# Attention with a block mask, then a gMLP: q and k transposed by TensorE into tiles whose mask rows stay, with earlier loads

## The chip, the core and the metric

The kernel runs on one core of a Trainium2 chip. The metric is the device time of one execution in microseconds, as the median of several executions. The core has five engines that run their own instruction streams in program order and meet through semaphores: TensorE (PE for its matmuls, PEld for its weight loads), VectorE (DVE), ScalarE (ACT), GpSimd (POOL) and SyncE (SP), which computes nothing here and issues most of the DMAs. Matmul results land in PSUM; the other tiles lie in SBUF. DMAs are issued from the queues of SP, ACT and POOL.

## The reference, cut to what matters

```python
# q, k, v: (4, 8, 768, 64) float32; sampled_blocks: (24, 3) integers
def _attn_ref(q, k, v, sampled_blocks):
    scores = scale * np.matmul(q, k.transpose(0, 1, 3, 2))     # scale = 1/8
    mask = np.abs(blk_i - blk_j) <= 1                          # blocks of 32 positions
    mask = mask | (blk_i == 0) | (blk_j == 0) | (blk_i == 23) | (blk_j == 23)
    for qb in range(24):
        for kb in sampled_blocks[qb]:
            mask[qb*32:(qb+1)*32, kb*32:(kb+1)*32] = True
    scores = np.where(mask, scores, -1e9)
    attn = softmax(scores)
    return np.matmul(attn, v)

def _moe_ref(x, w_in, w_spatial, b_spatial, w_out):            # x: (4, 768, 512), heads side by side
    h = np.maximum(x @ w_in, 0.0)                              # w_in: (512, 1024)
    u, v = h[..., :512], h[..., 512:]
    v_n = (v - mean(v)) / np.sqrt(var(v) + 1e-06)
    v_s = w_spatial @ v_n + b_spatial[None, :, None]           # w_spatial: (768, 768)
    return (u * v_s) @ w_out                                   # w_out: (512, 512)
```

The output is float32 of shape (4, 768, 512).

## The kernel before

Batches and heads are worked through in 16 pairs of heads (`NP`), four pairs a batch. A head has 768 positions, in 6 chunks (`NCH`) of 128. The main loop runs over pairs `p` and 12 steps `s`, six a head. A step emits `qk_exp`: two matmuls of 384 columns for the scores of one chunk of keys against all queries (L235), and one exponential by ScalarE out of PSUM (L239). Seven steps later (`LAG`) comes `av` for the same place: six matmuls of 65 columns (L251), the 65th column giving the sum of the exponentials. At a head's last chunk `norm` divides (VectorE, L264 and L265). Scores have two PSUM buffers (tag `sc`), so TensorE can be one step ahead of ScalarE.

The mask is made by the matmul itself. A contraction row is 88 long (`KR`): 64 of the head and 24, one a block of keys. On the k side, these 24 are 1 in the key's own block; on the q side they are 0 where the query's block may see the key's block and -300 where not. Before the change, they stand as columns behind the 64 of `nat_k` and `nat_q`, two tiles of each of [position, head, chunk, 128 columns], filled once: `key_blocks` (L169, L171) on POOL, `query_blocks` (L202) on VectorE.

For each pair, at step 0 of the pair before it, the loop emits: the loads of the pair after (`load`, L96; SP's queue, float32 staging tiles `st_q`, `st_k`, `st_v` with two buffers each), the casts to bfloat16 on POOL (`cast_qk`, L104, and `cast_v`, L113), and for k and for q one DMA transpose on SP's queue (`tr_dma`, L118), which turns the whole of `nat` into `t_k` or `t_q` with the contraction on the partitions. Pair 0 alone is transposed on TensorE (`tr_first`, L207 to L212). All three weights are loaded on POOL's queue at pair 0's step 0 (L430, L432, L434).

After step 8 of the next pair, `xtr` transposes a pair's normalized output to `xt`: by a DMA transpose on SP (L278), for the last pair of a batch on TensorE with a copy by VectorE (L274, L276). Then the batch's gMLP is queued as 24 units (`moe_units`), spread over the next 48 steps by a budget: six `v_unit` (L323; VectorE evicts at L329 and takes statistics at L332 and L333), six `u_unit` (L346), six `s_unit` (L368; a DMA transpose of `gn` to `gt` on SP behind each) and six `o_unit` (L386), whose results go to `osb`, four buffers, copied by ScalarE (L391) or VectorE (L393) in turn, and from there to the output by a DMA on SP (L394). Units use PSUM tag `moe`, two buffers, as do the transposes on TensorE. For the last batch the units run one after the other behind the loop. In pairs 2 and 3, six `wspt_unit` transpose the spatial weights (L287).

What sets the order is the program's own: each engine's queue has its instructions in the order in which the loop emits them, and an instruction that waits holds all that is behind it on its queue, DMAs on SP too.

Of the kernel before, what the change touches and what calls it, by code (L numbers as in the profile page):

```python
# [12 lines left out]
I32 = mybir.dt.int32  # L13
# [13 lines left out]
def kernel(  # L27
# [49 lines left out]

    nat = {nm: [const.tile([128, 2, NCH, 128], BF16, name=f"nat_{nm}{i}") for i in range(2)]
           for nm in "qk"}
# [12 lines left out]
    def load(p, names="qkv"):  # L92
        b, g = divmod(p, NG)
        for nm, src in (("q", q), ("k", k), ("v", v)):
            if nm in names:
                nc.sync.dma_start(out=st_tile(p, nm), in_=dram(src, b, 2 * g, 2))  # L96

    def cast_qk(p, nm, h, eng):
        src = st[nm, p][:, h].rearrange("p (c d) -> p c d", d=D)
        dst = nat[nm][p % 2][:, h, :, 0:D]  # L100
        if eng is nc.scalar:
            nc.scalar.activation(out=dst, in_=src, func=AF.Copy)
        else:
            eng.tensor_copy(out=dst, in_=src)  # L104
# [12 lines left out]
    def tr_dma(p, nm):  # L117
        nc.sync.dma_start_transpose(  # L118
            out=t_tile(p, nm).rearrange("x h (c n) -> x (h c) n", c=NCH),
            in_=nat[nm][p % 2].rearrange("p h c x -> p (h c x)"))  # L120
# [8 lines left out]
    load(0, "v")  # L129
    load(1)  # L130
    nc.sync.dma_start(out=b_col, in_=moe_b_spatial.rearrange("(p c) -> p c", c=NCH))

    nc.vector.memset(warm, 0.0)
# [32 lines left out]
    def key_blocks(i):  # L166
        x = nat["k"][i][:, :, :, D:KR]
        pat = [[0, 2], [1, NCH], [-BLK, NB]]
        nc.gpsimd.affine_select(out=x, in_=x, compare_op=ALU.is_ge, fill=0.0, base=0,  # L169
                                pattern=pat, channel_multiplier=NCH)  # L170
        nc.gpsimd.affine_select(out=x, in_=x, compare_op=ALU.is_ge, fill=0.0,  # L171
                                base=BLK - 1, pattern=[[0, 2], [-1, NCH], [BLK, NB]],
                                channel_multiplier=-NCH)

    key_blocks(0)
# [16 lines left out]
    cast_qk(0, "q", 0, nc.vector)  # L192
    cast_qk(0, "k", 0, nc.scalar)

    mq = psum.tile([128, 512], FP32, tag="av", bufs=2, name="mq")
    mq = mq[:, 0:NCH * NB].rearrange("p (c b) -> p c b", b=NB)
    for c in range(NCH):
        nc.tensor.matmul(out=mq[:, c, :], lhsT=ind[:, c * 128:(c + 1) * 128], rhs=bm,
                         start=True, stop=True)

    def query_blocks(i, h):
        nc.vector.tensor_copy(out=nat["q"][i][:, h, :, D:KR], in_=mq)  # L202

    def tr_first(h, nm, copy):
        ps = psum.tile([128, S], BF16, tag="moe", bufs=2)
        for c in range(NCH):
            nc.tensor.transpose(out=ps[:, c * 128:(c + 1) * 128], in_=nat[nm][0][:, h, c, :],  # L207
                                identity=ident)
        copy(qkt[nm, 0][0:KR, h, :], ps[0:KR, :])
# [20 lines left out]
    def qk_exp(j, ci):  # L230
# [3 lines left out]
        for hf in range(2):  # L234
            nc.tensor.matmul(out=ps[:, hf * 512:hf * 512 + HALF],  # L235
                             lhsT=qkt["k", j // 2][0:KR, j % 2, ci * 128:(ci + 1) * 128],
                             rhs=qkt["q", j // 2][0:KR, j % 2, hf * HALF:(hf + 1) * HALF],
                             start=True, stop=True)
# [65 lines left out]
    def moe_units(b):  # L304
# [75 lines left out]
        for tcc in range(NCH):  # L380
            def o_unit(tcc=tcc):
# [7 lines left out]
                osb = work.tile([128, DM], FP32, tag="osb", bufs=4)  # L389
# [15 lines left out]
    for p in range(NP + 1):  # L405
        for s in range(12):
# [6 lines left out]
            if p == 0 and s == 1:  # L413
                tr_first(1, "k", dve_copy)
                tr_first(1, "q", dve_copy)
            if s == 0 and p < NP:
                if p == 0:
                    cast_v(0)
                if p + 2 < NP:
                    load(p + 2)  # L420
                if p + 1 < NP:
                    if p == 0:
                        key_blocks(1)
                    for nm in "kq":
                        for h in range(2):
                            cast_qk(p + 1, nm, h, nc.gpsimd)
# [62 lines left out]
```

## Time and profile before

| what | us |
|---|---|
| median of 3 runs (265.31 to 266.99) | 265.33 |
| the profiled execution | 264.3 |
| its span, first to last instruction | 262.6 |
| PE busy | 221.6 |
| ACT busy | 171.6 |
| PEld busy | 131.1 |
| DVE busy | 103.8 |
| POOL busy | 57.3 |

A profile is of one execution. An engine's busy time says nothing of what it waits for: for this, the profile has a list of waits (who waited for whom), a timeline, and the chain of work that ended last. In rows of the timeline the numbers are the start and the length in us; then come the engine, the line, the operation, the output and inputs by the program's names, the shapes and how many were merged; in square brackets stands how long the engine was idle before, and what ended this. "SPq" is SP's queue of DMA issues, and its length that of issuing, not of moving the data.

### The profile page before, as it was taken

Reading aid. Unit: us, or ns where it says so; the run is one execution under the profiler, and the core shown is the slowest. Engines: PE = TensorE matmul, PEld = TensorE weight load, DVE = VectorE, ACT = ScalarE, POOL = GpSimd, SP = SyncE. Lnnn points to the kernel's source line nnn. Section 1 sums busy time; section 2 is a strip of 40 time slices with the busy share of each in tenths; the row PEclk is TensorE's granted clock in tenths of the full one; section 3 lists DMA queues with packets and bytes.
Section 4 is the critical chain, followed back from the end, with each engine's and each line's share of the span. In section 5 each row is a group of like instructions: output and inputs, shape, how many; then the busy total and the mean of one; then the engine's idle time right before and its main releaser. Section 6 shows DMA issues by size and latency. Waiting matters only on the chain.

```text
span 262.6 us, 5197 instructions
## 1 busy us (share of the span) xinstructions
PE 221.6 (84%) x2090; PEld 131.1 (50%) x2090; DVE 103.8 (40%) x228; ACT 171.6 (65%) x244; POOL 57.3 (22%) x116
## 2 busy tenths in 40 slices
PE   5880049999899999996699999993999999989994
PEld 1540026667656655563365655561455655544451
DVE  7500011323289324321487233330496233349442
ACT  3590029999977986786178976783279967526441
POOL 5761004304403520404015302104015000003000
PEclk9776557999999999999599999998599999999998
DMA  6499999999990957979972939789954332740006
GB/s 200 160 272 165 191 262 158 265 241 196 276 284 13 244 108 195 199 178 218 335 180 40 272 73 263 120 218 260 307 108 79 73 72 40 116 184 15 0 5 235
DMA packets 84379, 44.77 MB, mean 170 GB/s; under 512 B 67844, under 2 KB 80644, under 8 KB 84228
## 3 DMA queue, kind: packets, MB, share of 16 engines
q1 hardware_dynamic: 82832, 41.30, 66.4%
q0 software_dynamic: 1200, 2.75, 6.0%
q10 hardware_dynamic: 324, 0.39, 0.5%
q8 instruction: 16, 0.26, 0.4%
q14 instruction: 7, 0.06, 0.1%
HBM read 24.38 MB, written 6.29 MB: 117 GB/s over the span
## 4 chain that ended last, share of the span: by engine, by line
PE 62%; DMA 16%; ACT 8%; SPq 7%; POOL 2%; issue 2%; DVE 1%; POOLq 0%; DVEq 0%; ACTq 0%
PE ps L235 18%; PE ps_av L251 9%; PE ps_moe L368 9%; ACT a_all L239 8%; PE ps_moe L323 7%; DMA t_q<-nat_q 6%; PE ps_moe L346 6%; SPq L118 5%; DMA st_k<-in_k_dram 5%; PE ps_moe L386 3%; DMA out_dram<-osb 3%; DMA st_v<-in_v_dram 2%; PE ps_t L368 2%; PE ps_t L386 1%; PE ps_t L346 1%
## 5 line engine op out<-in xcount | busy, mean ns | idle before, releaser
L239 ACT ACTIVATE a_all<-ps 128x768 bf16<-128x768 f32 x192 | 144.5, 810 | 64.3 <-PE ps L235 63.8
L235 PE MATMUL ps<-t_q,t_k 88*128 88x384 bf16 x384 | 99.1, 342 | 23.6 <-DMA t_q<-nat_q 17.6
L251 PEld LDWEIGHTS <-a_all 128*128 128x128 bf16 x1152 | 64.2, 101 | 35.7 <-issue 5.3
L251 PE MATMUL ps_av<-vv,a_all 128*128 128x65 bf16 x1152 | 70.0, 197 | 0.0
L235 PEld LDWEIGHTS <-t_k 88*128 88x128 bf16 x384 | 29.4, 101 | 29.5 <-issue 26.3
L104 POOL CAST nat_k<-st_k 128x384 bf16<-128x384 f32 x30 | 14.5, 512 | 86.5 <-DMA st_k<-in_k_dram 64.9
L264 DVE RECIPROCAL rc<-ps_av 128x6 f32<-128x6 f32 x32 | 6.0, 186 | 63.2 <-PE ps_av L251 63.2
L323 PE MATMUL ps_moe<-w_in_t,xt 128*128 128x512 bf16 x72 | 21.1, 420 | 10.1 <-DVE osb L393 10.1
L371 DVE SCALAR_TENSOR_TENSOR gn<-ps_moe,b_col,un 128x512 bf16<-128x512 f32 x18 | 13.5, 750 | 32.7 <-PE ps_moe L368 32.7
L368 PE MATMUL ps_moe<-vn,w_spt 128*128 128x512 bf16 x108 | 26.3, 378 | 0.0
L368 PEld LDWEIGHTS <-w_spt 128*128 128x128 bf16 x144 | 13.8, 97 | 14.3
L323 PEld LDWEIGHTS <-xt 128*128 128x128 bf16 x96 | 9.9, 103 | 21.5 <-issue 13.2
L336 POOL TENSOR_SCALAR std<-mv 128x3 f32<-128x3 f32 x8 | 1.9, 242 | 83.5 <-DVE mv L333 72.1
L346 PE MATMUL ps_moe<-w_in_t,xt 128*128 128x512 bf16 x72 | 18.5, 378 | 0.0
L386 PE MATMUL ps_moe<-w_out_t,gt 128*128 128x512 bf16 x72 | 18.5, 378 | 0.0
L265 DVE TENSOR_TENSOR xn<-ps_av,rc 128x384 bf16<-128x384 f32 x32 | 17.8, 557 | 1.1
L332 DVE BATCH_NORM_STATS2 stats<-vsb 128x6 f32<-128x512 bf16 x24 | 16.7, 694 | 1.4 <-ACT vsb L327 0.8
L113 POOL CAST vv<-st_v 128x768 bf16<-128x768 f32 x16 | 13.5, 842 | 13.1 <-DMA st_v<-in_v_dram 8.3
L393 DVE COPY osb<-ps_moe 128x512 f32<-128x512 f32 x9 | 6.2, 691 | 25.4 <-PE ps_moe L386 13.3
L329 DVE TENSOR_SCALAR vsb<-ps_moe 128x512 bf16<-128x512 f32 x18 | 12.3, 684 | 7.9 <-PE ps_moe L323 7.9
L104 POOL CAST nat_q<-st_q 128x384 bf16<-128x384 f32 x30 | 14.4, 507 | 0.0
L346 PEld LDWEIGHTS <-xt 128*128 128x128 bf16 x96 | 9.3, 97 | 9.5
(80 smaller groups left out, 139.5 us busy)
## 6 DMA issues: line engine op xcount, KB each, us to landing
st_v<-in_v_dram SPq DMA_DIRECT2D x16, 384.0 KB, 5.1
out_dram<-osb SPq DMA_DIRECT2D x24, 256.0 KB, 2.1
st_q<-in_q_dram SPq DMA_DIRECT2D x15, 384.0 KB, 3.6
st_k<-in_k_dram SPq DMA_DIRECT2D x15, 384.0 KB, 4.3
ws_nat<-in_moe_w_spatial_dram POOLq DMA_DIRECT2D x1, 1152.0 KB, 12.5
w_in_t<-in_moe_w_in_dram POOLq DMA_DIRECT2D x1, 1024.0 KB, 17.5
w_out_t<-in_moe_w_out_dram POOLq DMA_DIRECT2D x1, 512.0 KB, 20.1
st_k<-in_k_dram ACTq DMA_DIRECT2D x2, 192.0 KB, 4.8
```

The source lines that it names most:

```text
L104: eng.tensor_copy(out=dst, in_=src)
L113: nc.gpsimd.tensor_copy(out=vv[p % 3][:, :, :, 0:D], in_=st.pop(("v", p)).rearrange("p h (c d) -> p h c d", d=D))
L235: nc.tensor.matmul(out=ps[:, hf * 512:hf * 512 + HALF], lhsT=qkt["k", j // 2][0:KR, j % 2, ci * 128:(ci + 1) * 128], rhs=qkt["q", j // 2][ ...
L239: nc.scalar.activation(out=a_ref[j][:, ci, :].rearrange("p (b c) -> p b c", b=2), in_=ps.rearrange("p (b c) -> p b c", b=2)[:, :, 0:HALF], ...
L251: nc.tensor.matmul(out=av_ref[j][:, qc, :], lhsT=a_ref[j][:, ci, qc * 128:(qc + 1) * 128], rhs=vv[p % 3][:, h, ci, :], start=(ci == 0), st ...
L265: nc.vector.tensor_tensor(out=xn_ref[p][:, :, h, :], in0=ps[:, :, 0:D], in1=rc.to_broadcast([128, NCH, D]), op=ALU.mult)
L323: nc.tensor.matmul(out=ps, lhsT=xt(g)[:, tcc * 128:(tcc + 1) * 128], rhs=w_in_t[:, g, DH:DFF], start=(g == 0), stop=(g == NDM - 1))
L332: nc.vector.bn_stats(out=stats, in_=vsb[:, tcc, :])
L346: nc.tensor.matmul(out=ps, lhsT=xt(g)[:, tcc * 128:(tcc + 1) * 128], rhs=w_in_t[:, g, 0:DH], start=(g == 0), stop=(g == NDM - 1))
L368: nc.tensor.matmul(out=ps, lhsT=w_spt[:, sc, tcc * 128:(tcc + 1) * 128], rhs=vn[:, sc, :], start=(sc == 0), stop=(sc == NCH - 1))
L371: nc.vector.scalar_tensor_tensor(out=gn[:, tcc, :], in0=ps, scalar=b_col[:, tcc:tcc + 1], in1=un[:, tcc, :], op0=ALU.add, op1=ALU.mult)
L386: nc.tensor.matmul(out=ps, lhsT=gt[:, tcc, dhc, :], rhs=w_out_t[:, dhc, :], start=(dhc == 0), stop=(dhc == NDH - 1))
```

## The change

- q and k of pairs 1 to 15 are transposed by TensorE. `tr_pair` does it for one pair and one of k and q: six transposes of [128 positions, two heads of 64], one a chunk, into one PSUM tile of tag `moe`, and two copies by VectorE of 64 partitions x 768, one a head. They are emitted at steps 5 (k) and 9 (q) of the pair before.
- `qt` and `kt` are four standing tiles each of 88 partitions, used in turn by head. Their last 24 partitions hold the mask and are written once: `kt`'s are the block indicators `ind`, `qt`'s are computed by two matmuls of 384 columns and copied by ScalarE; six copies by VectorE (`second_head`) bring both to the other three tiles. `nat` shrinks to the 64 columns of two heads side by side and loses its mask columns, their memsets, `key_blocks` and `query_blocks`.
- One cast on POOL takes both heads of q or k (`prepare`, with `cast_v`). It is emitted two pairs ahead at step 7, and the loads on SP three pairs ahead at step 7.
- The weights are issued on POOL at three places of the loop: `ws_nat` in pair 0 behind the casts of pair 1, `w_in_t` behind those of pair 2, `w_out_t` behind those of pair 3.
- `osb` has six buffers instead of four, `xt` eight instead of ten. The sampled blocks are loaded ahead of k of pair 0. One unit that is left at the loop's end runs ahead of the last `xtr`, not behind it.

```diff
-    nat = {nm: [const.tile([128, 2, NCH, 128], BF16, name=f"nat_{nm}{i}") for i in range(2)]
-           for nm in "qk"}
+    qt = [const.tile([KR, S], BF16, name=f"qt{s}") for s in range(4)]
+    kt = [const.tile([KR, S], BF16, name=f"kt{s}") for s in range(4)]
...
-    def load(p, names="qkv"):
+    def load(p, names="qkv", eng=nc.sync):
...
+                eng.dma_start(out=st_tile(p, nm), in_=dram(src, b, 2 * g, 2))
+
+    nat = {}
+
+    def nat_tile(p, nm):
+        nat[nm, p] = work.tile([128, NCH, 2, D], BF16, tag=f"nat_{nm}", bufs=2,
+                               name=f"nat_{nm}")
+
+    def cast_qk(p, nm, hs, eng):
+        src = st[nm, p][:, hs].rearrange("p h (c d) -> p h c d", d=D)
+        dst = nat[nm, p].rearrange("p c h d -> p h c d")[:, hs]
...
-    qkt = {}
-
-    def t_tile(p, nm):
-        qkt[nm, p] = work.tile([128, 2, S], BF16, tag=f"t_{nm}", bufs=3, name=f"t_{nm}")
-        return qkt[nm, p]
...
-    def tr_dma(p, nm):
-        nc.sync.dma_start_transpose(
-            out=t_tile(p, nm).rearrange("x h (c n) -> x (h c) n", c=NCH),
-            in_=nat[nm][p % 2].rearrange("p h c x -> p (h c x)"))
+    def prepare(p):
+        for nm in "kq":
+            nat_tile(p, nm)
+            cast_qk(p, nm, slice(0, 2), nc.gpsimd)
+        cast_v(p)
...
+    nc.scalar.dma_start(out=samp_i, in_=_listify(sampled_blocks).bitcast(I32))
     nc.scalar.dma_start(out=stk[:, 0:1], in_=dram(k, 0, 0, 1))
-    nc.scalar.dma_start(out=samp_i, in_=_listify(sampled_blocks).bitcast(I32))
...
-    for i in range(2):
-        nc.vector.memset(nat["k"][i][:, :, :, D:KR], 1.0)
-        for nm in "kq":
-            nc.vector.memset(nat[nm][i][:, :, :, KR:128], 0.0)
-        if i == 0:
-            nc.scalar.activation(out=tiny, in_=tiny, func=AF.Exp)
...
-    def key_blocks(i):
-        x = nat["k"][i][:, :, :, D:KR]
-        pat = [[0, 2], [1, NCH], [-BLK, NB]]
...
-    key_blocks(0)
...
+    nat_tile(0, "q"), nat_tile(0, "k")
+    cast_qk(0, "q", slice(0, 1), nc.vector)
+    cast_qk(0, "k", slice(0, 1), nc.scalar)
+    nc.vector.tensor_copy(out=kt[0][D:KR, :], in_=ind)
+
+    mq = psum.tile([128, 1024], FP32, tag="sc", bufs=2, name="mq")
+    for hf in range(2):
+        nc.tensor.matmul(out=mq[0:NB, hf * 512:hf * 512 + HALF], lhsT=bm,
+                         rhs=ind[:, hf * HALF:(hf + 1) * HALF], start=True, stop=True)
+    nc.scalar.activation(out=qt[0][D:KR, :].rearrange("p (b c) -> p b c", b=2),
+                         in_=mq[0:NB].rearrange("p (b c) -> p b c", b=2)[:, :, 0:HALF],
+                         func=AF.Copy)
...
+    def tr_head(h, nm, copy):
...
+            nc.tensor.transpose(out=ps[0:D, c * 128:(c + 1) * 128], in_=nat[nm, 0][:, c, h],
                                 identity=ident)
-        copy(qkt[nm, 0][0:KR, h, :], ps[0:KR, :])
-
-    def dve_copy(o, i):
-        nc.vector.tensor_copy(out=o, in_=i)
-
-    def act_copy(o, i):
-        nc.scalar.activation(out=o, in_=i, func=AF.Copy)
-
-    t_tile(0, "q"), t_tile(0, "k")
-    query_blocks(0, 0)
-    tr_first(0, "k", act_copy)
-    tr_first(0, "q", dve_copy)
-    cast_qk(0, "k", 1, nc.vector)
-    cast_qk(0, "q", 1, nc.vector)
-    query_blocks(0, 1)
-    query_blocks(1, 0)
-    query_blocks(1, 1)
+        copy((qt if nm == "q" else kt)[h][0:D, :], ps[0:D, :])
+
+    def tr_pair(p, nm):
+        src = nat.pop((nm, p))
+        ps = psum.tile([128, S], BF16, tag="moe", bufs=2)
+        for c in range(NCH):
+            nc.tensor.transpose(out=ps[:, c * 128:(c + 1) * 128],
+                                in_=src[:, c].rearrange("p h d -> p (h d)"), identity=ident)
+        for h in range(2):
+            nc.vector.tensor_copy(out=(qt if nm == "q" else kt)[(2 * p + h) % 4][0:D, :],
+                                  in_=ps[h * D:(h + 1) * D, :])
+
+    tr_head(0, "q", dve_copy)
+    tr_head(0, "k", dve_copy)
+
+    def second_head():
+        cast_qk(0, "k", slice(1, 2), nc.vector)
+        cast_qk(0, "q", slice(1, 2), nc.vector)
+        for sl in range(1, 4):
+            nc.vector.tensor_copy(out=kt[sl][D:KR, :], in_=kt[0][D:KR, :])
+            nc.vector.tensor_copy(out=qt[sl][D:KR, :], in_=qt[0][D:KR, :])
...
-                             lhsT=qkt["k", j // 2][0:KR, j % 2, ci * 128:(ci + 1) * 128],
-                             rhs=qkt["q", j // 2][0:KR, j % 2, hf * HALF:(hf + 1) * HALF],
+                             lhsT=kt[j % 4][:, ci * 128:(ci + 1) * 128],
+                             rhs=qt[j % 4][:, hf * HALF:(hf + 1) * HALF],
...
-        xt_ref[p] = work.tile([128, S], BF16, tag="xt", bufs=10, name="xt")
+        xt_ref[p] = work.tile([128, S], BF16, tag="xt", bufs=8, name="xt")
...
-                osb = work.tile([128, DM], FP32, tag="osb", bufs=4)
+                osb = work.tile([128, DM], FP32, tag="osb", bufs=6)
...
-            if p == 0 and s == 1:
-                tr_first(1, "k", dve_copy)
-                tr_first(1, "q", dve_copy)
-            if s == 0 and p < NP:
+            if p == 0 and s == 0:
+                second_head()
+            if p == 0 and s == 2:
+                tr_head(1, "k", dve_copy)
+                tr_head(1, "q", dve_copy)
+            if p + 1 < NP and s in (5, 9):
+                tr_pair(p + 1, "kq"[s // 8])
+            if p == 0 and s == 0:
+                cast_v(0)
+                prepare(1)
+                load(2)
+                nc.gpsimd.dma_start(out=ws_nat,
+                                    in_=moe_w_spatial.rearrange("(p c) s -> p c s", c=NCH))
+            if s == 7 and p + 2 < NP:
+                if p + 3 < NP:
+                    load(p + 3)
+                prepare(p + 2)
                 if p == 0:
-                    cast_v(0)
-                if p + 2 < NP:
-                    load(p + 2)
-                if p + 1 < NP:
-                    if p == 0:
-                        key_blocks(1)
-                    for nm in "kq":
-                        for h in range(2):
-                            cast_qk(p + 1, nm, h, nc.gpsimd)
-                        tr_dma(p + 1, nm)
-                    cast_v(p + 1)
-                if p == 0:
-                    nc.gpsimd.dma_start(out=ws_nat,
-                                        in_=moe_w_spatial.rearrange("(p c) s -> p c s", c=NCH))
                     nc.gpsimd.dma_start(out=w_in_t,
                                         in_=moe_w_in.rearrange("(g p) f -> p g f", p=128))
+                if p == 1:
                     nc.gpsimd.dma_start(out=w_out_t,
...
+    if moe_q:
+        moe_q.popleft()[1]()
     xtr(NP - 1)
     moe_q.extend(moe_units(B - 1))
```

Three places show how the instructions move. The first is SP's queue at the start, behind the loads of pairs 0 and 1 (the numbers are the tiles' own). Before:

```order
L96 DMA st_q_201<-in_q_dram 128x2x384
L96 DMA st_k_203<-in_k_dram 128x2x384
L96 DMA st_v_205<-in_v_dram 128x2x384
L118 DMA_TRANSPOSE t_k_211<-nat_k1_77 128x12x128
L118 DMA_TRANSPOSE t_q_215<-nat_q1_75 128x12x128
L96 DMA st_q_318<-in_q_dram 128x2x384
```

After the change, on the same queue and at the same place:

```order
L95 DMA st_q_202<-in_q_dram 128x2x384
L95 DMA st_k_204<-in_k_dram 128x2x384
L95 DMA st_v_206<-in_v_dram 128x2x384
L95 DMA st_q_263<-in_q_dram 128x2x384
L95 DMA st_k_265<-in_k_dram 128x2x384
L95 DMA st_v_267<-in_v_dram 128x2x384
```

The loads of pair 3 now follow those of pair 2 directly, without a transpose between them.

The second is SP's queue in pair 8, where the first batch's outputs stand. Before:

```order
L394 DMA out_0_dram<-osb_1565 128x512
L96 DMA st_q_1579<-in_q_dram 128x2x384
L96 DMA st_k_1581<-in_k_dram 128x2x384
L96 DMA st_v_1583<-in_v_dram 128x2x384
L118 DMA_TRANSPOSE t_k_1587<-nat_k1_77 128x12x128
L118 DMA_TRANSPOSE t_q_1591<-nat_q1_75 128x12x128
L394 DMA out_0_dram<-osb_1599 128x512
```

After the change, on the same queue in the same pair:

```order
L371 DMA_TRANSPOSE gt_1000<-gn_999 128x4x128
L390 DMA out_0_dram<-osb_1682 128x512
L390 DMA out_0_dram<-osb_1701 128x512
L390 DMA out_0_dram<-osb_1734 128x512
L390 DMA out_0_dram<-osb_1762 128x512
L390 DMA out_0_dram<-osb_1800 128x512
L95 DMA st_q_1816<-in_q_dram 128x2x384
```

Five outputs now follow one another, and the pair's loads come behind the fifth instead of the first.

The third is VectorE's queue in pair 4, from the last `xt` copy of the first batch to its first v_unit. Before:

```order
L264 RECIPROCAL rc<-ps_av 128x6
L265 TENSOR_TENSOR xn<-ps_av,rc 128x6x64
L276 COPY xt<-ps 128x768
L329 TENSOR_SCALAR vsb<-ps_moe 128x512
L332 BN_STATS stats<-vsb 128x6
```

After the change, on the same queue:

```order
L260 RECIPROCAL rc<-ps_av 128x6
L261 TENSOR_TENSOR xn<-ps_av,rc 128x6x64
L272 COPY xt<-ps 128x768
L210 COPY qt_76<-ps 64x768
L210 COPY qt_77<-ps 64x768
L325 TENSOR_SCALAR vsb<-ps_moe 128x512
```

Two copies of q of pair 5 now stand between the `xt` copy and the first v_unit's eviction.

More of the change, by code (lines that the diff above doesn't have):

```diff
@@ L128 @@
         nc.sync.dma_start(out=stq[:, h:h + 1], in_=dram(q, 0, h, 1))
-    load(0, "v")
-    load(1)
+    load(0, "v", nc.sync)
+    load(1, "qkv", nc.sync)
     nc.sync.dma_start(out=b_col, in_=moe_b_spatial.rearrange("(p c) -> p c", c=NCH))
-    nc.vector.memset(warm, 0.0)
     ind_nat = const.tile([NB, S], BF16)
@@ L140 @@
     nc.vector.memset(tiny, 0.0)
[L141 to L146 removed]
+    nc.vector.memset(warm, 0.0)
+    nc.scalar.activation(out=tiny, in_=tiny, func=AF.Exp)
     wps = psum.tile([128, 512], FP32, tag="moe", bufs=2)
@@ L191 @@
     nc.vector.tensor_copy(out=ind, in_=ind_nat.rearrange("b (p c) -> b c p", c=NCH))
[L192 to L208, printed above, removed]
-        copy(qkt[nm, 0][0:KR, h, :], ps[0:KR, :])
+    nat_tile(0, "q"), nat_tile(0, "k")
[9 more added lines that the diff above has]
+                         func=AF.Copy)
     def dve_copy(o, i):
```

12 lines of the change are left out of this document (3 added, 9 removed).

## The prediction

> **What bounds the kernel now.** I read the list of waits first, then the busy time by stage, then the timeline at the three places that these two point to. The list of waits (waiting line, releaser: total us, times, longest):
>
> ```profile
> PE ps L235 <- DMA t_q<-nat_q: 17.6, 2, 17.5
> DVE osb L393 <- DMA out_dram<-osb: 12.1, 2, 6.2
> PE ps_moe L323 <- DVE osb L393: 10.1, 2, 5.2
> ```
>
> TensorE stands still once for 17.5 us until a transposed q has landed, and twice for about 5 us behind a VectorE copy that waits for an output transfer. The stages (columns: stretch, its length, busy us and instructions of PE, PEld, DVE, ACT, POOL, granted TensorE clock, DMA share, GB/s), cut where a pair's first exponential starts:
>
> ```profile
> 18.89:37.37 18.48, 1.00 (x12) 0.57 (x9) 0.00 (x0) 0.81 (x2) 0.83 (x1) 0.58 1.14 191
> 37.37:65.73 28.36, 26.93 (x333) 19.03 (x331) 7.99 (x19) 26.66 (x37) 8.07 (x15) 0.91 1.08 224
> 65.73:112.95 47.22, 45.77 (x473) 27.86 (x472) 21.85 (x47) 38.94 (x55) 12.97 (x24) 1.00 0.78 186
> 112.95:132.55 19.60, 14.70 (x137) 8.52 (x135) 6.03 (x12) 10.09 (x15) 2.63 (x5) 0.83 1.00 256
> 132.55:169.98 37.43, 36.69 (x369) 21.88 (x366) 17.86 (x39) 30.14 (x43) 10.25 (x19) 1.00 0.70 156
> 169.98:190.22 20.24, 15.05 (x137) 8.54 (x136) 6.03 (x12) 10.09 (x15) 2.64 (x5) 0.83 0.99 254
> 190.22:227.20 36.98, 36.24 (x366) 21.64 (x363) 17.86 (x39) 29.70 (x43) 4.88 (x9) 1.00 0.43 75
> ```
>
> The first row is the end of pair 0, nearly empty. In the second (pairs 1 to 3, no gMLP work yet) ScalarE is busy for 26.66 of 28.36 us: it sets the pace. In the third, fifth and seventh TensorE is busy for 97 or 98%: there it sets the pace. The fourth and sixth are pairs 8 and 12, with holes. The timeline shows what makes the first hole:
>
> ```profile
> 13.67 12.49 SPq L118 DMA_TRANSPOSE t_k<-nat_k  x1
> 26.22 8.06 SPq L118 DMA_TRANSPOSE t_q<-nat_q  x1
> ```
>
> Two DMA transposes hold SP's queue for 20.5 us, until 34.28, and TensorE goes on when the second has landed. And the hole of pair 8:
>
> ```profile
> 116.81 2.66 SPq L118 DMA_TRANSPOSE t_k<-nat_k  x1
> 119.57 2.69 SPq L118 DMA_TRANSPOSE t_q<-nat_q  x1
> 122.35 5.05 SPq L394 DMA_DIRECT2D out_dram<-osb  x5
> 126.34 0.69 DVE L393 COPY osb<-ps_moe 128x512 f32<-128x512 f32 x1 [5.90 <-DMA out_dram<-osb]
> 127.09 1.86 PE L323 MATMUL ps_moe<-w_in_t,xt 128*128 128x512 bf16 x4 [4.90 <-DVE osb L393]
> ```
>
> Five outputs stand behind two transposes on SP; the fifth copy of a batch then has none of the four osb buffers, VectorE waits in order, and the xt copy that the next batch's first v_unit needs is behind it.
>
> **The change, part by part.**
>
> Removed: 30 DMA transposes. The first hole ends with them. The last exponential of pair 0 takes about 0.9 us to the next pair when nothing waits, so 18.48 - 0.9 = 17.6 us go. What pair 1 then needs is not late: its loads and casts were over long before (the casts of pair 2 start in the next fence's second row). Added there: two sets of six transposes for pair 1, on a TensorE that ScalarE paces; 0 us if all fits, 0.84 us each as a set of six lasted at the low clock. I take 0.25 each.
>
> ```profile
> 9.43 0.84 PE L207 MATMUL ps<-ident,nat_k 128*128 128x128 bf16 x6
> 16.60 0.96 POOL L104 CAST nat_k<-st_k 128x384 bf16<-128x384 f32 x2 [1.36 <-DMA st_k<-in_k_dram]
> 119.27 0.35 PE L251 MATMUL ps_av<-vv,a_all 128*128 128x65 bf16 x6
> 119.46 0.49 PE L235 MATMUL ps<-t_q,t_k 88*128 88x384 bf16 x2
> 119.79 0.36 PE L251 MATMUL ps_av<-vv,a_all 128*128 128x65 bf16 x6
> 121.17 0.35 PE L251 MATMUL ps_av<-vv,a_all 128*128 128x65 bf16 x6
> 121.36 0.50 PE L274 MATMUL ps<-ident,xn 128*128 128x128 bf16 x6
> 121.70 0.49 PE L235 MATMUL ps<-t_q,t_k 88*128 88x384 bf16 x2
> 42.22 7.95 ACT L239 ACTIVATE a_all<-ps 128x768 bf16<-128x768 f32 x11 [0.16 <-PE ps L235]
> 38.34 0.81 ACT L239 ACTIVATE a_all<-ps 128x768 bf16<-128x768 f32 x1 [0.16 <-PE ps L235]
> 39.30 0.81 ACT L239 ACTIVATE a_all<-ps 128x768 bf16<-128x768 f32 x1 [0.16 <-PE ps L235]
> 56.50 1.51 ACT L239 ACTIVATE a_all<-ps 128x768 bf16<-128x768 f32 x2 [0.41 <-PE ps L235]
> 111.47 0.87 PE ps_moe L386 x4
> ```
>
> The price of a set: without transposes, the score matmuls start 0.19 us after the attention-times-value matmuls (119.27 to 119.46), with six transposes between them 0.53 us (121.17 to 121.70). So a set costs 0.34 us of a TensorE that is the bound, 0.057 us a transpose. One step of attention costs TensorE 0.52 us (119.27 to 119.79) and ScalarE 7.95 / 11 = 0.72 us, so in pairs 0 to 3 there is 0.20 us of slack a step; a set costs between 0 and 0.34 us there, and I take the middle, 0.17.
>
> Pairs 1 to 3: six sets, +1.0 us. The first five exponentials of pair 1 came 0.96 us apart (38.34, 39.30) at the low clock that the hole had left (the stage's mean is 0.91); at 0.72, -1.2 us. At the start of pair 3 ScalarE waited 0.41 us for scores whose t_q had landed late, and at that of pair 4 likewise: -0.8. Together -1.0.
>
> Pairs 4 to 7: eight sets, one of them under ScalarE: 7 x 0.34 + 0.17 = +2.55. Pairs 9 to 11: six sets, +2.05. Pairs 13 to 15: four sets, since the last pair prepares nothing, +1.35. Pairs 8 and 12: two sets each, +0.7 each.
>
> The holes of pairs 8 and 12. Undisturbed, such a pair is twelve steps of 0.52, five o_units and two v_units of four matmuls, 0.87 us each (the last row above, of the chain that ended last), and one set for xt: 6.24 + 6.1 + 0.34 = 12.7 us. Against 19.60 and 20.24 us that frees 6.9 and 7.5. On SP's queue, five outputs now go ahead of the loads and no transpose of q or k is left, and six buffers cover a whole batch's outputs, so that VectorE needs none of them back before the xt copy. A load can hold the queue only if its staging buffer is not yet cast, which then happened a pair earlier.
>
> VectorE gets 60 copies of 64x768 from PSUM. None ran before; the nearest is the first row below, 0.55 us for as many columns. That is 33 us on an engine busy for 104 of 263, but not everywhere:
>
> ```profile
> L276 DVE COPY xt<-ps 128x768 bf16<-128x768 bf16 x4 | 2.2, 552 | 1.6 <-PE ps L274 1.6
> 75.57:83.10 7.53, 7.53 (x79) 4.48 (x76) 6.92 (x16) 5.84 (x8) 1.13 (x2) 1.00 0.58 127
> ```
>
> While the v_units run, VectorE is busy for 6.92 of 7.53 us, and each set adds 1.1. Its lag keeps TensorE waiting only when it exceeds what two moe buffers cover, about one unit and two steps (0.87 + 2 x 0.52 = 1.9 us), and the u_units behind need VectorE little. Bounds 0 and 3.3 us a batch (three sets uncovered); near the lower end, 0.2 for each of three batches: +0.6.
>
> POOL: two casts of 384 columns become one of 768, about the same time (0.96 us for two, above). Its four mask operations go. The start: VectorE loses six memsets and four mask copies, gets one mask copy ahead of the first scores and k's copy, which was ScalarE's; ScalarE copies the query mask instead; seven more mask copies run while ScalarE works through head 0. The chain to the first exponential keeps its length within a set's copy (0.55 us) either way: 0. The last: TensorE waited 0.88 us for xn ahead of the last xt, and one output unit of 0.87 us now stands there. But that unit covered the xt copy behind it, 0.55 us, with VectorE's output copy now ahead of it: between -0.9 and +0.7, I take -0.2.
>
> ```profile
> 232.91 0.51 PE L274 MATMUL ps<-ident,xn 128*128 128x128 bf16 x6 [0.88 <-DVE xn L265]
> ```
>
> The sum: 262.6 - 17.6 + 0.5 - 1.0 + 2.55 - 6.9 - 7.5 + 1.4 + 2.05 + 1.35 + 0.6 - 0.2 = 237.85 us of span. The profiled execution took 264.3 us, 1.7 more than its span, which gives 239.6; the median of the runs is 265.33, 1.0 above that. Between the two I forecast **240.0 us**.
>
> **The rivals.**
>
> (a) Outputs still late. Another wait on SP ahead of the outputs (the xt and gt transposes stay there) keeps one or both holes of pairs 8 and 12: 240 + 7 = 247, or 254. For it: SP stays in order. Against: the rows of pair 8 show 5.35 us of transposes there and nothing else as long.
>
> (b) Loads late. With SP free, the loads of pairs 2 and 3 go out while weights land, and weights crowd them out:
>
> ```profile
> 12.69 0.42 SPq L96 DMA_DIRECT2D st_k<-in_k_dram  x1
> 13.20 0.42 SPq L96 DMA_DIRECT2D st_v<-in_v_dram  x1
> 14.47 0.77 POOL L434 DMA_DIRECT2D w_out_t<-in_moe_w_out_dram  x1
> 23.75 0.83 POOL L113 CAST vv<-st_v 128x768 bf16<-128x768 f32 x1 [5.29 <-DMA st_v<-in_v_dram]
> ws_nat<-in_moe_w_spatial_dram POOLq DMA_DIRECT2D x1, 1152.0 KB, 12.5
> w_out_t<-in_moe_w_out_dram POOLq DMA_DIRECT2D x1, 512.0 KB, 20.1
> ```
>
> v of pair 2 took 10 us beside them, against 3.9 for k (12.69 to 16.60). The Trainium skill (DMA: Bandwidth & Descriptors, on queues, rings and completion order) says that each DMA engine goes round its queues packet by packet; the trace agrees, since one load beside large weight packets took 10 us. POOL runs ahead of the loop: it issues w_in as soon as v of pair 2 is cast, about 23 us, and w_out after v of pair 3. TensorE wants k of pair 3 at pair 2's step 5, about 37.4 - 17.1 + 8.9 + 3.6 = 32.8 us. With ws_nat landed by 25 it is there; if all three weights pass first (20.1 us after 14.5, so 34.6, and two casts) it is 36.5, a stall of 4 us and a low clock after it: 245.
>
> (c) VectorE bounds the v_units: the upper end above, 3 x 3.3 us: 249.
>
> (d) Slower: transposes that do not overlap. If each holds TensorE for the whole duration that its row gives, 180 of them cost 180 x 0.219 = 39.4 instead of 10.2 us: 269.
>
> ```profile
> L274 PE MATMUL ps<-ident,xn 128*128 128x128 bf16 x24 | 2.0, 219 | 0.9 <-DVE xn L265 0.9
> ```
>
> It decides from about 0.2 us a transpose. Against it: the same row has 24 in 2.0 us, 0.083 each, and the step above 0.057. The Trainium skill (TensorE: Matmul & The Clock Gate, Part 4: PE-mode transpose) gives about 275 ns for one in a kernel's context; by that as an occupancy the sum would be an estimated 279. The trace disagrees with such a reading.
>
> **How the numbers follow.** Forecast 0.68 (its own range 236 to 244: 9 x 0.17 = 1.5 us for the sets under ScalarE, 0.6 for the start, 0.8 for the end, 1.0 for the time that the sum is set against); (a) 0.11; (b) 0.08; (c) 0.08; (d) 0.03; something else 0.02. A range of 235 to 248 takes in (b), one hole of (a) and most of (c). A measurement of this kernel can tell about 1% from no change: faster by over 1% is everything but (d) and half of the rest, 0.95; within 1% 0.02; slower 0.03.
>
> **What would show it.** No wait of TensorE on a DMA near 19 us; the next pair's first exponential about 20 us from the start; pairs 8 and 12 near 13.4 us; pairs 5 to 7 0.7 us longer each; VectorE's busy time near 135 us, TensorE's clock low only in the first 20 us. Wrong would be: a wait of the transposes on POOL's casts (b), of moe matmuls on VectorE's copies (c), of osb on the output DMA (a), or sets far longer than 0.34 us (d).

## The result, and the profile after

The changed kernel takes 237.24 us, the median of four runs (235.59 to 239.17), against 266.13 us (265.31 to 266.99) for the kernel before beside it: a ratio of 0.889, with a 95% interval from 0.883 to 0.896. Ratios here and below leave out executions that took over 1.5% more than the fastest of the same kernel (of these four the longest, 239.17 us); medians are of all.

The profile is of the execution of 239.17 us (span 237.2). It can be read all the same: in the later profiles of this kernel and of the variants that change only its first pair, its buffers or its weights, each pair from the second on has the same length to within about 0.2 us, and what differs lies in pair 0 and ahead of it. Stages of the changed kernel, cut where a pair's first exponential starts (columns as in the prediction's stages):

```profile
0.00:8.54 8.54, 6.28 (x26) 2.75 (x27) 4.36 (x16) 2.81 (x4) 2.90 (x17) 1.00 0.74 236
8.54:21.63 13.09, 10.23 (x84) 6.60 (x83) 8.10 (x14) 9.09 (x13) 5.79 (x7) 0.74 0.70 176
21.63:48.57 26.94, 25.96 (x363) 19.57 (x362) 14.43 (x31) 26.32 (x37) 9.68 (x13) 1.00 1.11 264
48.57:97.97 49.40, 48.24 (x522) 30.39 (x520) 31.05 (x63) 39.37 (x56) 11.83 (x16) 1.00 0.40 115
97.97:111.48 13.51, 13.51 (x149) 8.52 (x148) 8.32 (x16) 10.20 (x16) 2.43 (x3) 1.00 0.93 247
111.48:150.34 38.86, 38.49 (x403) 23.66 (x400) 24.78 (x51) 30.50 (x43) 9.63 (x13) 1.00 0.38 106
150.34:163.85 13.51, 13.51 (x149) 8.51 (x148) 8.32 (x16) 10.19 (x15) 2.43 (x3) 1.00 0.94 248
163.85:201.93 38.08, 37.53 (x389) 22.82 (x386) 22.30 (x47) 30.06 (x43) 4.83 (x7) 1.00 0.20 46
201.93:237.20 35.27, 31.00 (x201) 15.21 (x198) 17.56 (x35) 14.11 (x24) 2.31 (x4) 0.98 0.25 94
```

The empty stretch of pair 0 is gone, and pairs 8 and 12 (rows five and seven) have TensorE busy throughout. From pair 4 to the loop's end TensorE is busy for 97% or more. One stretch still looks wrong: pair 0 (row two) is 13.09 us long at a mean clock of 0.74, while each of pairs 1 to 3 takes 9. The list of waits within this stretch (8 to 20 us), TensorE's own rows from the longest:

```profile
PE ps L207 <- DVE kt L191: 1.7, 1, 1.7
PE ps L231 <- ACT a_all L235: 1.1, 2, 0.6
```

In the whole list TensorE waits for no DMA any more. Behind pair 0 it is held behind VectorE's copies of q and k only at the first v_unit of a batch (its weight loads, 1.1 us in three waits). SP's and VectorE's rows of pair 8, where the outputs had been stuck:

```profile
98.49 7.28 SPq L390 DMA_DIRECT2D out_dram<-osb  x5
106.72 0.69 DVE L389 COPY osb<-ps_moe 128x512 f32<-128x512 f32 x1 [0.93 <-PE ps_moe L382]
107.33 0.55 DVE L272 COPY xt<-ps 128x768 bf16<-128x768 bf16 x1
```

Five outputs now go out as they come, spread over 7.3 us, and the sixth output copy, the one that had no buffer before, waits for its matmul, not for a transfer.

Stage by stage, what was forecast and what came (the stages of the two profiles subtracted; the parts of the sum put together by stage):

| stage | before | after | change | forecast |
|---|---|---|---|---|
| up to the first exponential | 9.03 | 8.54 | -0.5 | 0 |
| pair 0 | 28.34 | 13.09 | -15.3 | -17.1 |
| pairs 1 to 3 | 28.36 | 26.94 | -1.4 | -1.0 |
| pairs 4 to 7 | 47.22 | 49.40 | +2.2 | +2.75 |
| pair 8 | 19.60 | 13.51 | -6.1 | -6.2 |
| pairs 9 to 11 | 37.43 | 38.86 | +1.4 | +2.25 |
| pair 12 | 20.24 | 13.51 | -6.7 | -6.8 |
| pairs 13 to 15 | 36.98 | 38.08 | +1.1 | +1.55 |
| behind the loop | 35.40 | 35.27 | -0.1 | -0.2 |

### The profile page after: what moved, and what is told of

It reads as the page before. It is cut to its first block, busy times and chain, and to the rows that moved or that the text cites. A ratio compares the mean times of both kernels' runs of the same rounds, so it can differ in the third digit from the quotient of the medians.

```text
span 237.2 us, 5509 instructions
## 1 busy us (share of the span) xinstructions
PE 224.8 (95%) x2266; PEld 138.0 (58%) x2266; DVE 139.2 (59%) x286; ACT 172.6 (73%) x244; POOL 51.8 (22%) x82
## 3 DMA queue, kind: packets, MB, share of 16 engines
q0 software_dynamic: 1200, 2.75, 6.8%
## 4 chain that ended last, share of the span: by engine, by line
PE 80%; ACT 12%; DMA 3%; DVE 3%; issue 1%; ACTq 0%
PE ps L231 22%; PE ps_av L247 12%; ACT a_all L235 12%; PE ps_moe L364 10%; PE ps_moe L319 7%; PE ps_moe L382 7%; PE ps_moe L342 7%; PE ps L207 4%; DMA st_k<-in_k_dram 3%; PE ps_t L364 2%; PE ps_t L319 2%; PE ps_t L382 1%; PE ps_t L342 1%; PE ps_sc L364 1%; DVE qt L221 1%; PE ps_sc L382 1%
## 5 line engine op out<-in xcount | busy, mean ns | idle before, releaser
L231 PE MATMUL ps<-qt,kt 88*128 88x384 bf16 x384 | 95.1, 330 | 4.8 <-ACT a_all L235 3.7
L247 PEld LDWEIGHTS <-a_all 128*128 128x128 bf16 x1152 | 61.8, 99 | 30.9 <-issue 1.4
L247 PE MATMUL ps_av<-vv,a_all 128*128 128x65 bf16 x1152 | 68.5, 195 | 0.0
L231 PEld LDWEIGHTS <-kt 88*128 88x128 bf16 x384 | 28.3, 99 | 9.1 <-issue 6.1
L210 DVE COPY kt<-ps 64x768 bf16<-64x768 bf16 x30 | 16.5, 551 | 18.1 <-PE ps L207 17.9
L210 DVE COPY qt<-ps 64x768 bf16<-64x768 bf16 x30 | 16.6, 554 | 8.9 <-PE ps L207 8.2
L109 POOL CAST nat_k<-st_k 128x768 bf16<-128x768 f32 x15 | 12.4, 829 | 28.7 <-DMA st_k<-in_k_dram 28.7
L319 PE MATMUL ps_moe<-w_in_t,xt 128*128 128x512 bf16 x72 | 18.5, 379 | 0.0
L342 PE MATMUL ps_moe<-w_in_t,xt 128*128 128x512 bf16 x72 | 18.5, 378 | 0.0
L382 PE MATMUL ps_moe<-w_out_t,gt 128*128 128x512 bf16 x72 | 18.5, 378 | 0.0
L319 PEld LDWEIGHTS <-xt 128*128 128x128 bf16 x96 | 8.9, 97 | 9.8 <-DVE kt L210 1.1
L342 PEld LDWEIGHTS <-xt 128*128 128x128 bf16 x96 | 9.2, 97 | 9.1
L109 POOL CAST nat_q<-st_q 128x768 bf16<-128x768 f32 x15 | 13.2, 879 | 2.9 <-issue 2.9
```

Of the source, the lines that this page charges most:

```text
L210: nc.vector.tensor_copy(out=(qt if nm == "q" else kt)[(2 * p + h) % 4][0:D, :], in_=ps[h * D:(h + 1) * D, :])
L231: nc.tensor.matmul(out=ps[:, hf * 512:hf * 512 + HALF], lhsT=kt[j % 4][:, ci * 128:(ci + 1) * 128], rhs=qt[j % 4][:, hf * HALF:(hf + 1) * ...
L247: nc.tensor.matmul(out=av_ref[j][:, qc, :], lhsT=a_ref[j][:, ci, qc * 128:(qc + 1) * 128], rhs=vv[p % 3][:, h, ci, :], start=(ci == 0), st ...
L319: nc.tensor.matmul(out=ps, lhsT=xt(g)[:, tcc * 128:(tcc + 1) * 128], rhs=w_in_t[:, g, DH:DFF], start=(g == 0), stop=(g == NDM - 1))
L342: nc.tensor.matmul(out=ps, lhsT=xt(g)[:, tcc * 128:(tcc + 1) * 128], rhs=w_in_t[:, g, 0:DH], start=(g == 0), stop=(g == NDM - 1))
L382: nc.tensor.matmul(out=ps, lhsT=gt[:, tcc, dhc, :], rhs=w_out_t[:, dhc, :], start=(dhc == 0), stop=(dhc == NDH - 1))
```

## The experiments

**Which cure closed the holes of pairs 8 and 12?** The change did two things there: it took the transposes off SP and added two buffers. Each is undone or done alone.

```diff
-                osb = work.tile([128, DM], FP32, tag="osb", bufs=6)
+                osb = work.tile([128, DM], FP32, tag="osb", bufs=4)
```

> The changed kernel with four osb buffers again. Theory: the holes of pairs 8 and 12 came from outputs that stood behind the DMA transposes of q and k; with none there, output 2 of a batch has landed before copy 6 wants its buffer, so nothing returns: 236 to 239 us, pairs 8 and 12 within 0.5 us of 13.5. Rival: the two added buffers are what closed the holes: then 5 to 7 us come back in each, 248 to 251 us.

```diff
 (the kernel before)
-                osb = work.tile([128, DM], FP32, tag="osb", bufs=4)
+                osb = work.tile([128, DM], FP32, tag="osb", bufs=6)
```

> The kernel before with six osb buffers and nothing else. Theory: either cure is enough by itself, since copy 6 then needs no buffer back and VectorE goes straight on to the xt copy: pairs 8 and 12 at about 12.7 us, 265 - 6.9 - 7.5 = 251 us. Rival: with SP's queue still held by the transposes another wait takes their place (outputs and loads late): 258 us or more.

The changed kernel with four buffers took 237.6 us (0.896 of the kernel before, 0.890 to 0.902), no different from six. The kernel before with six took 254.55 us (0.964, 0.957 to 0.970). Stages of pairs 8 and 12, first of the changed kernel with four buffers, then of the kernel before with six:

```profile
96.77:110.22 13.45, 13.45 (x149) 8.46 (x148) 8.26 (x16) 10.17 (x16) 2.43 (x3) 1.00 0.91 240
149.14:162.59 13.45, 13.45 (x149) 8.46 (x148) 8.26 (x16) 10.17 (x16) 2.43 (x3) 1.00 0.74 213
```

```profile
114.13:127.02 12.89, 12.87 (x137) 7.87 (x136) 6.24 (x13) 9.96 (x16) 2.63 (x5) 1.00 1.02 241
164.41:177.58 13.17, 12.87 (x137) 7.87 (x136) 6.52 (x13) 9.96 (x15) 2.63 (x5) 1.00 1.00 238
```

Either cure closes both holes by itself; the two added buffers are worth nothing once SP is free. In the kernel before, that one number would have brought 3.6%. Its median lies 3.5 us above the expected 251, and the cause of that stays open: the profiled execution (251.61 us) was the fastest of the four and doesn't show it.

**What made the hole of pair 0?** The kernel before, with its weights spread over the loop:

```diff
 (the kernel before)
+                if p == 1:
                     nc.gpsimd.dma_start(out=w_in_t,
...
+                if p == 2:
                     nc.gpsimd.dma_start(out=w_out_t,
```

> The kernel before with its weights at three places of POOL's queue: the spatial weights in pair 0 as before, the input weights behind the casts that pair 1 emits, the output weights behind those that pair 2 emits. Theory: the 17.5 us hole came from weights that crowded out the 256-byte packets of the DMA transposes, so that they held SP for 20.5 us instead of some 5; with only the spatial weights in flight the hole shrinks to 6 to 9 us, and some of it comes back in pairs 1 and 2: 256 to 262 us. Rival: the transposes were slow or late by themselves, and the hole stays above 14 us: 263 us or more.

It took 265.59 us, 1.006 of the kernel before (1.001 to 1.011): no gain, where 256 to 262 us had been expected. The stages of pairs 0 to 3, and SP's transposes of k for pairs 1 to 4 (the profiled execution took 268.89 us):

```profile
9.60:31.80 22.20, 11.16 (x71) 6.46 (x70) 1.40 (x4) 9.29 (x12) 8.01 (x15) 0.81 0.89 165
31.80:45.07 13.27, 10.01 (x102) 6.54 (x100) 1.50 (x4) 9.19 (x13) 3.31 (x6) 0.76 1.13 214
45.07:59.10 14.03, 11.10 (x119) 7.74 (x117) 3.18 (x7) 9.21 (x12) 2.63 (x5) 0.74 1.17 200
59.10:70.11 11.01, 10.70 (x122) 7.65 (x120) 3.31 (x8) 9.19 (x12) 2.69 (x5) 0.75 0.93 217
```

```profile
14.23 9.72 SPq L118 DMA_TRANSPOSE t_k<-nat_k  x1
30.57 7.74 SPq L118 DMA_TRANSPOSE t_k<-nat_k  x1
45.73 7.13 SPq L118 DMA_TRANSPOSE t_k<-nat_k  x1
58.52 2.95 SPq L118 DMA_TRANSPOSE t_k<-nat_k  x1
```

Each of the three that had a piece of the weights beside it held SP for 7 to 10 us, the one without for 2.95. The place of the cause was right, the size of the effect not: the hole was cut in three, pair 0's part fell from 17.5 to about 11 us and the rest came back in pairs 1 and 2, 13 to 14 us long instead of 9 to 10. In neither of the two arrangements that were run could the DMA transposes of q and k share the first 45 us with the weights (5.5 MB, float32 in HBM) without holding up TensorE. A run without any weights beside the transposes was not made.

**Does the spacing of the weights matter after the change?**

```diff
             if p == 0 and s == 0:
...
                 nc.gpsimd.dma_start(out=ws_nat, ...)
+                nc.gpsimd.dma_start(out=w_in_t, ...)
+                nc.gpsimd.dma_start(out=w_out_t, ...)
             if s == 7 and p + 2 < NP:
...
-                if p == 0:
-                    nc.gpsimd.dma_start(out=w_in_t, ...)
-                if p == 1:
-                    nc.gpsimd.dma_start(out=w_out_t, ...)
```

> The changed kernel with all three weights issued at one place, pair 0's step 0, as before. Theory: q and k of pair 3 are then behind 20 us of weight packets; they were cast at 28 to 30 us in the changed kernel and are wanted at about 34, so TensorE waits at pair 2's step 5 for 1 to 5 us, and longer for pair 4: 238 to 244 us, with a wait of the transposes on POOL's casts in the list. Rival: the loads go through between the weight packets and nothing waits: within 1 us of the changed kernel.

It took 237.53 us (0.902, 0.896 to 0.908), as the changed kernel, and not the expected 238 to 244. The output weights needed longer from issue to landing, 22.1 us against 12.0, but landed earlier, since they were issued at 14.0 us instead of 30.6; and nothing on TensorE's path came too late. POOL's cast of k of pair 3, and the output weights' time to landing:

```profile
29.74 0.83 POOL L109 CAST nat_k<-st_k 128x768 bf16<-128x768 f32 x1 [11.38 <-PE ps L231]
w_out_t<-in_moe_w_out_dram POOLq DMA_DIRECT2D x1, 512.0 KB, 22.1
```

k of pair 3 was cast by 30.6 us and wanted at about 32; its cast had waited for TensorE, not for its load. So the early loads or the missing transposes are what mattered, and no run tells these two apart; the three spaced pieces are worth nothing by themselves.

**What do the sets of transposes cost?** First without the sets of pairs 2 to 15, then with their transposes but without VectorE's copies (except for one pair's):

```diff
-            if p + 1 < NP and s in (5, 9):
+            if p + 1 < NP and s in (5, 9) and p > 0:
+                nat.pop((("kq"[s // 8]), p + 1))
+            elif p + 1 < NP and s in (5, 9):
                 tr_pair(p + 1, "kq"[s // 8])
```

> The changed kernel without the transposes and copies of pairs 2 to 15 (the scores of these pairs are made from q and k of pairs 0 and 1). Theory: a set costs 0.34 us where TensorE is the bound and 0 to 0.2 where ScalarE is; by the stages of the two profiles 28 sets cost about 7 us in all: 229 to 231 us. Rival one: nearly all are hidden: 235 or more. Rival two: they cost their whole duration or VectorE's time, 15 us or more: 222 or less.

```diff
     def tr_pair(p, nm):
...
-        for h in range(2):
+        for h in range(2 if p == 1 else 0):
             nc.vector.tensor_copy(...)
```

> The changed kernel with the transposes of pairs 1 to 15 but with VectorE's copies of them only for pair 2; scores of the other pairs are made from the tiles that are there. Theory: TensorE pays for the sets and VectorE's copies are covered, but for the first v_unit of a batch: 1 us or less under the changed kernel, pair 5 within 0.3 us of 12.4. Rival: VectorE's time is the price (the statistics and the copies queue up while the v_units run): pairs 5, 9 and 13 fall back towards 11.6 us, 3 to 7 us less in all.

The copies that stayed in the second are those of pair 1, not of pair 2 as the expectation says; those of pairs 2 to 15 are left out. Without the sets: 229.9 us (0.868, 0.863 to 0.874), 7.3 us under the changed kernel's median, as expected. Its stages from pair 1 on:

```profile
20.73:47.42 26.69, 25.31 (x333) 18.00 (x330) 7.97 (x19) 26.11 (x38) 8.41 (x11) 1.00 1.12 236
47.42:94.63 47.21, 45.76 (x473) 27.84 (x472) 22.30 (x47) 38.93 (x55) 11.80 (x16) 1.00 0.44 133
94.63:107.34 12.71, 12.71 (x137) 7.80 (x136) 6.10 (x12) 9.96 (x15) 2.43 (x3) 1.00 0.75 229
107.34:144.71 37.37, 36.64 (x367) 21.84 (x365) 18.24 (x39) 30.15 (x43) 9.35 (x13) 1.00 0.43 122
144.71:157.42 12.71, 12.71 (x137) 7.79 (x136) 6.09 (x12) 9.96 (x15) 2.43 (x3) 1.00 0.91 285
157.42:194.34 36.92, 36.19 (x365) 21.59 (x362) 18.13 (x39) 29.69 (x43) 4.62 (x7) 1.00 0.24 39
```

Taken from the changed kernel's stages, 28 sets cost 0.25 (six sets in pairs 1 to 3), 2.2 (eight), 0.8, 1.5 (six), 0.8 and 1.2 us (four): 6.7 us, 0.24 a set. Where ScalarE sets the pace they are nearly free (0.04 each). The stretch of pair 7 in which k's set runs shows that this goes on behind pair 4 (ScalarE's row, then TensorE's, of the changed kernel):

```profile
89.27 2.25 ACT L235 ACTIVATE a_all<-ps 128x768 bf16<-128x768 f32 x3 [0.98 <-PE ps L231]
89.59 0.50 PE L207 MATMUL ps<-ident,nat_k 128*128 128x128 bf16 x6
```

Behind an s_unit, three exponentials follow without a pause, 0.75 us each, and the set runs under them. Against the run without sets, pairs 6 and 7 grew by about 0.3 us each, pair 5 (v_units and u_units) and pair 8 (o_units and v_units) by 0.8: about one of the two sets in each of pairs 6 and 7 is hidden.

Without the copies it took 236.61 us (0.898, 0.889 to 0.906), 0.6 under the changed kernel and within the spread. Pair 5 of it, with the v_units:

```profile
57.60:69.82 12.22, 12.22 (x132) 7.58 (x129) 9.84 (x22) 10.10 (x14) 4.56 (x7) 1.00 0.09 17
```

12.22 us against 12.38 with the copies, and nearly the same difference in pairs 9 and 13; pair 4 is 0.06 us shorter, the others are equal. So VectorE's 31 us (56 copies of 0.55) are covered but for about 0.5 us in all.

**What makes pair 0 long?** Two suspects: VectorE's mask copies, behind which the eviction of a moe buffer stands, and the clock.

```diff
-        for sl in range(1, 4):
-            nc.vector.tensor_copy(out=kt[sl][D:KR, :], in_=kt[0][D:KR, :])
-            nc.vector.tensor_copy(out=qt[sl][D:KR, :], in_=qt[0][D:KR, :])
+    def masks(sl):
+        nc.vector.tensor_copy(out=kt[sl][D:KR, :], in_=kt[0][D:KR, :])
+        nc.vector.tensor_copy(out=qt[sl][D:KR, :], in_=qt[0][D:KR, :])
...
             if p == 0 and s == 2:
...
+                masks(1)
+            if p == 0 and s in (6, 7):
+                masks(s - 4)
```

> The changed kernel with the six mask copies of the second_head step moved behind the copies of head 1 of pair 0 (tile 1 at step 2, tiles 2 and 3 at steps 6 and 7). Theory: in pair 0 TensorE waits 1.7 us for a moe buffer whose eviction stands behind these copies on VectorE; it ends, and pair 0 shrinks from 13.1 to about 11.2 us: 2 us less than the changed kernel, 235 us. Rival: the low clock in pair 0 or late casts bind there anyway: less than 0.7 us.

237.66 us (0.896, 0.892 to 0.901): no gain in time, though the wait of 1.7 us was gone from its list. In its profile pair 0 takes 11.01 us, as the theory had it (11.2). But the profile with four `osb` buffers, whose mask copies stand where the change put them, has 11.54. The two stages, late copies first:

```profile
8.21:19.22 11.01, 10.04 (x84) 6.41 (x83) 6.21 (x13) 8.95 (x12) 5.71 (x7) 0.69 0.69 201
8.87:20.41 11.54, 10.85 (x84) 6.60 (x83) 7.32 (x13) 9.12 (x12) 5.22 (x7) 1.00 0.72 185
```

With the copies in place, pair 0 took from 11.2 to 13.1 us in six profiles, so what moving them is worth can't be told from this spread. The clock of 1.00 in the second row is not to be taken at its word: the two score matmuls of a step take 0.80 us in it up to 17 us and 0.49 from 18.5 us on, the lengths that go with the low and with the full clock in the other profiles. The column shows no low clock there; the lengths do. The second suspect, then:

```diff
+            if p == 0 and s < 7:
+                fill = psum.tile([128, 512], FP32, tag="av", bufs=2, name="fill")
+                nc.tensor.matmul(out=fill[:, 0:HALF], lhsT=warm[:, 0:128], rhs=warm[:, 0:HALF],
+                                 start=True, stop=True)
             if p == 0 and s == 0:
                 second_head()
```

First with the moved mask copies:

> The changed kernel with the mask copies moved as in the run before, and one extra matmul of 384 columns in each of pair 0's first seven steps, whose result is not used. Theory: the low clock in pair 0 comes of TensorE being busy for less than half of these steps (0.33 of 0.72 us); with 0.49 of 0.72 us it stays high as in pair 1 (0.52 of 0.72), pair 0 falls from 11 to 13 us to 9 to 9.7, the spread of the runs shrinks, and the median falls by 1.5 to 3 us, to 234.5 to 236. Rival: the clock falls for another reason (the waits at the start), and the extra matmuls at the low clock cost 0.25 us a step: 237 to 240.

235.34 us (234.77 to 236.34). To compare it with the changed kernel on one chip, three more ran side by side: the changed kernel, the extra matmuls alone, and both.

> The changed kernel once more, beside the next two on the same chip, so that they can be compared with it. All theories: 235.5 to 239 us, with everything behind pair 0 as in its first profile to 0.1 us a pair, and pair 0 between 11 and 13.1 us.

> The changed kernel with the seven extra matmuls in pair 0 and with the mask copies where the change put them. Theory: the clock is what makes pair 0 long and the mask copies cost at most 1 us of it, since at the full clock TensorE reaches the step 5 transposes earlier and waits for their moe buffer longer: pair 0 at 9.8 to 11 us, median 235.5 to 237. Rival: the extra matmuls alone do it: pair 0 at 9.4 to 9.6, median as the run with both.

> The kernel with both (extra matmuls in pair 0, mask copies moved), a second time. Theory: 1 to 3 us less than the changed kernel on the same chip, with pair 0 at 9.3 to 9.7 us. Rival: the gain of its first run was the chip's: no difference beyond the spread.

Medians: 238.07 us for the changed kernel (0.897, 0.892 to 0.903), 236.8 for the extra matmuls alone (0.897, 0.891 to 0.904), 235.07 for both (0.888, 0.883 to 0.893). The pair 0 stages, in this order; for both, from its first run:

```profile
7.61:20.32 12.71, 11.40 (x84) 7.02 (x83) 7.92 (x14) 9.16 (x12) 7.39 (x9) 0.60 0.75 211
8.55:17.86 9.31, 8.53 (x91) 5.55 (x90) 6.00 (x14) 8.73 (x12) 4.73 (x6) 1.00 0.60 181
7.37:16.77 9.40, 8.60 (x91) 5.57 (x90) 6.71 (x14) 8.74 (x12) 4.98 (x7) 1.00 0.68 217
```

With seven extra matmuls the granted clock reads 1.00, the two score matmuls of a step keep to 0.48 to 0.50 us, and pair 0 takes 9.3 to 9.6 us, with or without moved copies; for the extra matmuls alone that is the rival's stage, not the theory's 9.8 to 11. Without them it takes 11.0 to 13.1 us, with TensorE at the low clock for a part of it. So the low clock is the larger part of what made pair 0 long, and at the full clock the place of the mask copies makes no difference. That more work for TensorE in pair 0's first steps keeps the clock up is shown by this; at what load it falls is not, nor why it falls at different times (score matmuls take 0.80 us from 8.5 us on in the repeated run, and still 0.48 at 12 us in the first profile). In all three profiles with extra matmuls the clock was up by the first scores; the profile with four buffers shows that it need not be. On one chip, the kernel with both took 235.07 us against the changed kernel's 238.07, about 1%; the intervals of the ratios overlap by a little. Its first run, on another chip, gave 0.894 of the kernel before there, no less than the changed kernel's 0.889 in its own first run. The extra matmuls alone gave the shorter pair 0 too, but their times spread from 235.33 to 239.48, so their own gain in time stays open.

## Why the prediction was right, point by point

- The holes. Nearly the whole of the gain is where the prediction put it, and by its mechanism: no transposes on SP, no wait of TensorE on t_q, no output stuck. Pairs 8 and 12 came out 0.1 us from the forecast. That the buffers and the free queue are each enough was not in it; it counted them together. The signs that it named came: no wait on a DMA, pair 1's first exponential at 21.6 us (about 20 said), VectorE busy for 139 us (135 said).
- Pair 0: the mis-sized term. "I take 0.25 each" for its two sets, and the rest of the pair as before, gave -17.1, a pair 0 of 11.2 us; it was -15.3, or 13.1 us. In this profile TensorE waits 1.7 us in it for VectorE's copies and runs at the low clock from about 14 us on; in the other profiles with the same pair 0 it took 11.2 to 12.8, and with the extra matmuls, at the full clock, 9.3 to 9.6. So the forecast lies at the low end of a spread that it didn't foresee: it named the low clock of the first 20 us as what one would see, and put no price on it.
- The first exponential: forecast unchanged within one copy (0.55 us), came 0.5 us earlier here, but at 7.4 to 8.9 us in the other profiles of this kernel and its variants, so up to 1.7 us earlier.
- The price of a set, 0.34 us "of a TensorE that is the bound", holds within 0.06: in pair 8 two cost 0.80. "The middle, 0.17" under ScalarE was too much: 0.04. And the prediction took every set but one from pair 4 on as uncovered, while about two of the six in pairs 5 to 7 are free beside s_units. In all 28 sets and their copies cost 6.7 us against 8.95 that the terms for them make (1.0 + 2.55 + 0.7 + 2.05 + 0.7 + 1.35, and 0.6 for VectorE).
- These errors have opposite signs: +1.8 for pair 0, -2.25 for the sets, -0.5 for the start and +0.3 for what pairs 1 to 3 gain without their sets (26.69 against 28.36, where 2.0 was taken). That the span came out at 237.2 where 237.85 was forecast is thus partly luck; the large terms, the three holes, came by their mechanism. The time forecast, 240.0, was 2.8 above the median.
- VectorE, "+0.6" for its lag: the run without copies puts it at about 0.5 for the three batches. Right.
- The rivals. (a), outputs late: no wait of osb on an output transfer is left in pairs 8 and 12. (b), loads late: all three weights at once changed nothing. (c), VectorE: the copies are covered. (d), transposes that hold TensorE for their whole duration: 0.40 us for six where TensorE is the bound (pair 8), not 1.3.

## What to carry to other kernels

A queue that is served in order passes its delays on: five outputs were late because of two transposes that had nothing to do with them, and two more buffers, one number, would have cured that without the rest of the change. Moving a transpose from the DMA queue to a TensorE that is 84% busy can pay if the price is read between neighbours in the timeline (0.06 us each) and not from the duration of one (0.22 us), and it is nearly free where another engine sets the pace (0.04 us a set in pairs 1 to 3). When a stage is longer than its steps explain, look at the granted clock and at the length of one matmul ahead of the waits: here a few useless matmuls in a stretch with little work for TensorE took 3 us off a stage of 13.

## What was not expected of the hardware

The clock fell with TensorE at work. In pair 0 of the changed kernel the longest wait of TensorE was 1.7 us, yet the mean granted clock of the stage was 0.74 and 0.60 in its two profiles, and 1.00 with seven extra matmuls of 384 columns. The Trainium skill (TensorE: Matmul & The Clock Gate, Part 1: The HAM clock gate) names idle stretches of about 3.4 us as what brings the half clock; here no single idle stretch was that long, and the clock fell all the same.

VectorE's copies of mask rows from SBUF to SBUF took 0.34 us alone and about 0.97 us beside POOL's casts. VectorE's rows and POOL's at 10.5 us of the changed kernel:

```profile
10.52 0.34 DVE L220 COPY kt<-kt 24x768 bf16<-24x768 bf16 x1
10.78 0.99 DVE L221 COPY qt<-qt 24x768 bf16<-24x768 bf16 x1
```

```profile
10.73 0.83 POOL L109 CAST nat_k<-st_k 128x768 bf16<-128x768 f32 x1 [1.00 <-DMA st_k<-in_k_dram]
```

The second copy begins as the cast does, and takes 0.65 us more. The Trainium skill (SBUF — State Buffer, section on its two separate sides) says that the two engines share one pair of ports, which one holds for a whole instruction while the other waits; the trace agrees: the copy ends 0.2 us after the cast (11.77 against 11.56).

Last, the time outside the span was 1.7 to 2.2 us in 42 of the 50 executions of the changed kernel and its variants. In the other eight it was 2.3 to 3.6 us, for example in one with the extra matmuls alone (236.54 us with a span of 232.9). All eight are of the kernels with late mask copies, with extra matmuls or with both. What it is stays open; it is as large as the gains of these experiments, so that spans and medians have to be read together there.
